# Front of a fused Fourier-mixing and hardswish kernel: two DMA queues for x and filters, weights' bits ahead, last-stage loads in three steps, zero matmuls in the wait

**Chip, cores, metric.** One core of a Trainium2 chip. The time is the device time of one execution in microseconds (us), median over repeated runs.

## The reference

```python
def _attn_ref(x, filt_r, filt_i):                 # x: (8, 3008, 256)
    X = np.fft.rfft(x, axis=1)
    Y = X * (filt_r + 1j * filt_i)[None, :, :]
    return np.fft.irfft(Y, n=x.shape[1], axis=1).astype(np.float32)

def _moe_ref(x, w_in, w_out):                     # x: (24064, 256), w_in: (256, 2048)
    h = x @ w_in
    g = h * np.clip(h + 3.0, 0.0, 6.0) / 6.0
    return (g @ w_out).astype(np.float32)
```

The first result, as (8 * 3008, 256), is the second's input. Everything is float32.

## The kernel before

The Fourier transforms are matmuls with tables. A batch goes through: transform of x (for the first batch `a0_unit`, for the others `a_unit` and a trip of z through DRAM), filter units (`b_unit`, `f_unit`, `bi_unit`) with a trip of g through DRAM, and the last stage (`t4_load`, `n_unit`), which gives tokens to the hardswish steps. The float weights are rebuilt from their bits by `convert`, mostly on VectorE. Later batches' work is laid among the hardswish steps by `places`. What the change touches (`# ...` marks cuts):

```python
    def x0_load(j, n):                # batch 0's x, in five pieces of columns
        for p, a, m, h in ((0, 0, 32, 0), (H1, 0, 32, 1), (32, 32, NA - 32, 0), (H1 + 32, 32, NA - 32, 1),
                           (NA, 0, H1 - NA, 0)):
            nc.sync.dma_start(x0[p:p + m, j:j + n, :], rows[a:a + m, ds(h * HC + j, n), :])

    def z_store(b, c, q=None):
        # ...
                (q or nc.gpsimd).dma_start(z[:, :, ds(c * XC + 2 * g, 2), :], t[p0:p0 + KH, :, :, :])

    # ... the front:
        for c in range(FB):
            table_load(0, c)          # filters and tables, all on nc.sync
        for j in range(0, HC, 4):
            a0_unit(j)
        for c in range(FB, NT):
            table_load(0, c)
            convert(0, most=min(c + 2, 6))      # only loads bits
        convert(3, False, 6)
        # ...
        for c in range(NT + 1):
            # ... b_unit, f_unit of 2c, 2c+1
            if c:
                bi_unit(0, 2 * c - 2)
                g_store(0, 2 * c - 2, nc.scalar)
            if c == NT - 2:
                for i in range(2):
                    t4_load(i, 0, KH - 2 * TC)
        for i in range(2):
            t4_load(i, KH - 2 * TC, KH, (nc.sync, nc.scalar))
        convert(2, False)
        for i in range(2):
            for dh in range(2):
                n_unit(i, dh)
    # ... places of batch 1, in steps of about 8 us:
                b_at = [11 + 18 * i // 11 for i in range(NU)]
    # ...
                at(s, z_store, n, c, nc.sync if n == 1 else None)
    # ... the last output stores:
        po, qs = st["po", k], (nc.sync, nc.scalar, nc.gpsimd)
```

## Time and profile before

2763.46 us (2762.95 to 2768.56, 3 runs). The marks, from the trace (us from the start of the span):

| mark | before |
|---|---|
| batch 0's transform ends on TensorE | 29.51 |
| its filter stage ends | 67.74 |
| first last-stage matmul | 80.03 |
| first hardswish on VectorE | 90.20 |
| 21st hardswish (the weight conversions end at 150.3, with the 13th) | 184.41 |
| 23rd hardswish, after the wait for batch 1's z | 200.70 |
| 49th hardswish | 304.62 |
| last arithmetic on VectorE ends | 2753.55 |
| end of the span | 2763.09 |

How to read it: the same instruction, counted by its order, is sought in two traces, and the difference of its start is carried from mark to mark. Where the difference changes, time was won or lost; where it stays, nothing happened, however busy the engines were. Half clock means a stretch in which the trace shows a granted clock of 0.5; a matmul of the code is two passes in the trace (the 16 matmuls of zeros are x32).

### The profile page before, as it was taken

The page shows a single profiled execution, that of the slowest core. Times are in us where ns is not written, and L with a number is a line of the kernel's source. Part 1 is how long each engine was busy: PE and PEld are TensorE (multiplying, and loading weights), DVE is VectorE, ACT ScalarE, POOL GpSimd, SP SyncE. Part 2 cuts the span into 40 slices and gives each one's busy share as a digit, 9 for nine tenths or more (in the row PEclk, how much of TensorE's full clock was granted, in tenths as well). Part 3 has the DMA queues.
Part 4 walks back from the last instruction along what each step waited for, and adds up shares of the span by engine and source line. Part 5 has one row for each costly group of instructions (what it writes and reads, how often), then busy time and mean ns, then how long its engine had stood idle before and what let it go on. Part 6 is the DMA issues. An engine that isn't in the chain of part 4 may idle for free.

```text
span 2763.1 us, 47097 instructions
## 1 busy us (share of the span) xinstructions
PE 2708.6 (98%) x18122; PEld 2409.1 (87%) x18122; DVE 1941.5 (70%) x3399; ACT 1332.5 (48%) x2665; POOL 373.6 (14%) x585
## 2 busy tenths in 40 slices
PE   8789999999999999999999999999999999999998
PEld 6468888999889998899889998899988999999997
DVE  5747765777667776677756787567775777766665
ACT  4334455444554445544554445544455444444443
POOL 1311112010210102110121101210012100100000
PEclk9899999999999999999999999999999999999999
DMA  8632223221332213322133212332123321110000
GB/s 214 190 87 83 71 64 80 74 76 52 83 89 61 72 40 89 88 72 57 46 84 90 76 49 54 86 93 67 46 61 89 97 64 45 35 32 23 19 9 16
DMA packets 119145, 195.25 MB, mean 71 GB/s; under 512 B 21539, under 2 KB 82947, under 8 KB 118463
## 3 DMA queue, kind: packets, MB, share of 16 engines
q1 hardware_dynamic: 98703, 146.59, 18.8%
q0 software_dynamic: 16480, 42.13, 6.7%
q10 hardware_dynamic: 3738, 3.52, 0.5%
q8 instruction: 143, 2.34, 0.4%
q14 instruction: 81, 0.66, 0.1%
HBM read 120.32 MB, written 71.83 MB: 70 GB/s over the span
## 4 chain that ended last, share of the span: by engine, by line
PE 93%; DVE 3%; DMA 2%; SPq 0%; issue 0%; ACT 0%; POOL 0%; POOLq 0%; DVEq 0%; ACTq 0%
PE po L526 41%; PE al L450 23%; PE be L450 17%; PE psn L425 4%; PE psf L355 3%; PE psf L332 2%; PE psf L387 2%; DMA w_all<-in_x_dram 0%; PE po L300 0%; DMA w_all<-wb_t 0%; DVE g L500 0%; DVE y L230 0%; PE po L548 0%; PE al L537 0%; DVE y L243 0%
## 5 line engine op out<-in xcount | busy, mean ns | idle before, releaser
L526 PEld LDWEIGHTS po<-w_all,g 128*128 128x128 f32 x10304 | 1369.1, 192 | 143.5 <-issue 36.5
L526 PE MATMUL po<-w_all,g 128*128 128x128 f32 x10304 | 1399.3, 276 | 3.7 <-DVE g L500 3.3
L500 DVE SCALAR_TENSOR_TENSOR g<-r,h 128x512 f32<-128x512 f32 x736 | 506.4, 688 | 268.1 <-ACT r L495 255.5
L495 ACT ACTIVATE r<-h,half_c 128x512 f32<-128x512 f32 x736 | 531.2, 722 | 326.8 <-DVE h L476 314.8
L450 PE MATMUL al<-xt,w_all 128*128 128x256 f32 x2208 | 660.5, 381 | 1.5 <-DVE h L481 1.0
L476 DVE TENSOR_TENSOR h<-be,s 128x512 f32<-128x512 f32 x368 | 254.2, 691 | 271.3 <-PE be L450 259.9
L450 PE MATMUL be<-xn,w_all 128*128 128x256 f32 x1472 | 438.3, 379 | 0.0
L450 PEld LDWEIGHTS al<-xt,w_all 128*128 128x128 f32 x2208 | 335.5, 192 | 3.5 <-issue 2.2
L450 PEld LDWEIGHTS be<-xn,w_all 128*128 128x128 f32 x1472 | 280.0, 190 | 38.0
L490 ACT ACTIVATE h<-al 128x256 f32<-128x256 f32 x368 | 141.4, 384 | 350.5 <-PE al L450 350.5
L481 DVE TENSOR_TENSOR h<-al,s 128x256 f32<-128x256 f32 x368 | 156.3, 425 | 166.1 <-PE al L450 164.8
L508 DVE TENSOR_TENSOR g<-g 128x512 f32<-128x512 f32 x368 | 254.7, 692 | 12.7
L471 ACT ACTIVATE s<-al 128x256 f32<-128x256 f32 x368 | 141.4, 384 | 207.1 <-PE al L450 207.1
L462 ACT ACTIVATE s<-be 128x256 f32<-128x256 f32 x368 | 141.4, 384 | 176.3 <-PE be L450 176.3
L450 PE MATMUL al<-xn,w_all 128*128 128x256 f32 x736 | 219.9, 381 | 0.5 <-ACT h L490 0.5
L450 PE MATMUL be<-xt,w_all 128*128 128x256 f32 x736 | 218.9, 379 | 0.0
L461 ACT ACTIVATE s<-al 128x256 f32<-128x256 f32 x368 | 141.4, 384 | 70.9 <-PE al L450 70.9
L510 DVE TENSOR_TENSOR g<-g 128x256 f32<-128x256 f32 x368 | 160.8, 437 | 12.5
L344 POOL DMA_DIRECT2D z_tmp<-t x192 | 111.1, 587 | 411.3 <-ACT t L335 409.1
L507 DVE TENSOR_TENSOR g<-g 128x256 f32<-128x256 f32 x368 | 156.4, 425 | 12.6
L450 PEld LDWEIGHTS be<-xt,w_all 128*128 128x128 f32 x736 | 139.8, 190 | 18.9
L425 PEld LDWEIGHTS psn<-wai,t 128*128 128x128 f32 x1024 | 134.2, 195 | 20.2 <-issue 14.1
(114 smaller groups left out, 1770.1 us busy)
## 6 DMA issues: line engine op xcount, KB each, us to landing
t<-g_tmp SPq DMA_DIRECT2D x188, 120.0 KB
t<-z_tmp SPq DMA_DIRECT2D x42, 512.0 KB
g_tmp<-t POOLq DMA_DIRECT2D x84, 256.0 KB, 3.8
z_tmp<-t POOLq DMA_DIRECT2D x192, 96.0 KB, 3.3
out_dram<-o SPq DMA_DIRECT2D x321, 47.0 KB
xs<-in_x_dram SPq DMA_DIRECT2D x112, 128.0 KB
ft<-in_filt_r_dram SPq DMA_DIRECT2D x88, 128.0 KB
ft<-in_filt_i_dram SPq DMA_DIRECT2D x88, 128.0 KB
```

The source lines that it names most:

```text
L425: nc.tensor.matmul(ps[:, ts(q, TOK)], t4[i % 2][:, q, ts(dh, P)], wai[:, chunks[i][1] + q, :], start=True, stop=True)
L450: nc.tensor.matmul(ps, w_in[p][:, w, :], x, start=start, stop=stop, skip_group_check=True)
L461: nc.scalar.activation(out=s[:, 0, :], in_=al, func=AXT.Copy)
L462: nc.scalar.activation(out=s5, in_=be[:, 1, :], func=AXT.Copy)
L476: nc.vector.tensor_tensor(out=st["h"][0].rearrange("p (a n) -> p a n", a=2), in0=be, in1=s, op=ALU.add)
L481: nc.vector.tensor_tensor(out=st["h"][1][:, 256:512], in0=al, in1=s5, op=ALU.add)
L495: nc.scalar.activation(out=r, in_=st["h"][i], func=AXT.Relu, bias=half_c, scale=1.0 / 6.0)
L500: nc.vector.scalar_tensor_tensor(out=st["g", k, p][:, o:o + 2, :].rearrange("p a n -> p (a n)"), in0=st["r", i], scalar=1.0, in1=st["h"][i ...
L507: v.tensor_tensor(out=g[:, G1, :], in0=g[:, G3, :], in1=g[:, G22, :], op=ALU.add)
L508: v.tensor_tensor(out=g[:, G3:G2 + 1:2, :], in0=g[:, G3:G1 + 1, :], in1=g[:, G11:G11 + 1, :].broadcast_to([P, 2, 256]), op=ALU.subtract)
L510: v.tensor_tensor(out=g[:, G4, :], in0=g[:, G12, :], in1=g[:, G2, :], op=ALU.subtract)
L526: nc.tensor.matmul(st["po", k][bank][:, part, u, :], g[:, a, ts(u, P)], w_out[p][:, w, :], start=(p == 0 and n in OPENS and u == 0), stop= ...
```

## The change

Its intent is to fill TensorE's idle time in the first 200 us: x and filters issued from two queues (SyncE and GpSimd), five weights' bits loaded ahead, last-stage loads in three steps of k, 16 matmuls of zeros to keep the clock up in the wait for them, and batch 1's z stored from GpSimd's queue instead of SyncE's. The core of the diff (its renamings, the shape of t4, the moved sums, the warm-up, the first loads on ScalarE and the new place of the turns are cut):

```diff
+    def table_load(b, c, qs=(nc.sync, nc.sync)):
...
     def x0_load(j, n):
-        for p, a, m, h in ((0, 0, 32, 0), (H1, 0, 32, 1), ...
-            nc.sync.dma_start(x0[p:p + m, j:j + n, :], rows[a:a + m, ds(h * HC + j, n), :])
+        nc.vector.memset(x0[32:64, j:j + n, :], 0.0)
+        for a, m in (0, 32), (32, NA - 32):
+            for h, q in ((0, nc.sync), (1, nc.gpsimd)):
+                q.dma_start(x0[h * 64 + a:h * 64 + a + m, j:j + n, :], rows[a:a + m, ds(h * HC + j, n), :])
...
         for c in range(FB):
-            table_load(0, c)
+            table_load(0, c, two)                    # two = (nc.sync, nc.gpsimd)
         for j in range(0, HC, 4):
             a0_unit(j)
+        convert(3, False, 5)
         for c in range(FB, NT):
-            table_load(0, c)
-            convert(0, most=min(c + 2, 6))
-        convert(3, False, 6)
+            table_load(0, c, two)
+        convert(0, most=8)
...
             if c:
                 bi_unit(0, 2 * c - 2)
-                g_store(0, 2 * c - 2, nc.scalar)
-            if c == NT - 2:
-                for i in range(2):
-                    t4_load(i, 0, KH - 2 * TC)
-        for i in range(2):
-            t4_load(i, KH - 2 * TC, KH, (nc.sync, nc.scalar))
+                g_store(0, 2 * c - 2, (nc.scalar, nc.scalar) if c < NT else (nc.scalar, nc.sync))
+            if c > 3:
+                t4_load(0, (0, KH - 2 * TC, KH - TC)[c - 4], (KH - 2 * TC, KH - TC, KH)[c - 4], (nc.sync, nc.scalar)
+                        if c == NT else None, 1)
+        keep_warm(16)
         convert(2, False)
...
-                b_at = [11 + 18 * i // 11 for i in range(NU)]
+                b_at = [12 + 17 * i // 11 for i in range(NU)]
...
-                at(s, z_store, n, c, nc.sync if n == 1 else None)
+                at(s, z_store, n, c)
```

## The prediction

> **What bounds the kernel now.** I read the page first. Part 1 gives TensorE 98% of the span, and the 40 slices in part 2 are at 9 from the fourth on, so nearly everything is TensorE-bound and only the front can give time back.
>
> ```profile
> span 2763.1 us, 47097 instructions
> ...
> PE   8789999999999999999999999999999999999998
> ```
>
> Next I read the table of stretches for five long stages. Between 700 and 2700 us TensorE is busy all the time (500.00 of 500.00 in each stretch); between 200 and 700 us it lacks 7 us. This steady part, untouched by the diff except through batch 1's places, I take as fixed. What is saved in front is then saved at the end.
>
> Then I read the same table in stretches of 5 us (columns: length, then busy us of PE, PEld, DVE, ACT, POOL with counts, granted clock, DMA share, GB/s).
>
> ```profile
> 20.00:25.00 5.00, 5.00 (x40) 5.00 (x40) 0.00 (x0) 3.69 (x5) 0.00 (x0) 0.84 0.99 219
> ...
> 40.00:45.00 5.00, 5.00 (x32) 3.49 (x30) 4.30 (x8) 2.17 (x4) 0.00 (x0) 1.00 0.26 53
> ...
> 70.00:75.00 5.00, 0.00 (x0) 0.00 (x0) 4.86 (x9) 0.00 (x0) 1.86 (x3) 0.78 0.53 144
> 75.00:80.00 5.00, 0.00 (x0) 0.00 (x1) 0.37 (x1) 0.00 (x0) 1.36 (x3) 0.50 0.21 51
> ```
>
> See three things: the DMA engines are saturated at only about 219 GB/s early on; they nearly stop at 40 to 45 us; TensorE stands still from 67.8 to 80 us and its clock falls to half. The timeline gives the edges:
>
> ```profile
> 16.92 12.58 PE L300 MATMUL po<-p,w_all 110*128 110x128 f32 x96 [2.35 <-DMA w_all<-in_x_dram]
> ...
> 65.32 2.42 PE L387 MATMUL psf<-h,wi 128*64 128x512 f32 x8 [0.72 <-ACT t L390]
> ...
> 80.03 4.98 PE L425 MATMUL psn<-wai,t 128*128 128x94 f32 x22 [12.29 <-DMA t<-g_tmp]
> ...
> 89.24 2.21 PE L537 MATMUL be<-xn,w_all 128*128 128x512 f32 x4
> 90.20 0.69 DVE L500 SCALAR_TENSOR_TENSOR g<-r,al 128x512 f32<-128x512 f32 x1 [14.84 <-ACT r L495]
> ```
>
> So batch 0's first transform runs to 29.5 us, its filter stage to 67.74, TensorE waits 12.3 us for the loads of the last stage, and the first hardswish is at 90.2. From there to 150.4 VectorE is busy 56.2 of 60.2 us, converting the other eleven weight parts: this stage is VectorE-bound and only starts earlier or later as a whole. After it one stall remains, which the waits and the timeline show:
>
> ```profile
> 171.66 11.95 SPq L603 DMA_DIRECT2D out_dram<-o  x14
> 183.65 3.22 SPq L344 DMA_DIRECT2D z_tmp<-t  x4
> 190.23 1.49 SPq L348 DMA_DIRECT2D t<-z_tmp  x3
> ...
> 194.14 2.07 PE L355 MATMUL psf<-t,wb 128*128 128x256 f32 x4 [5.51 <-DMA t<-z_tmp]
> ```
>
> The last z stores of batch 1 stand on SyncE's queue behind fourteen output stores, the z load behind them, and TensorE waits 5.5 us for it.
>
> **What the Trainium skill says.** (1) "SBUF — State Buffer", Door 1: The DMA port swizzle: 32 or 64 partitions from 0 reach half of the 16 ports, at most about 218 GB/s. The trace agrees: 219 GB/s at a DMA share of 0.99 while x and filters come in pieces of at most 32 partitions. (2) The same page, "Can I just issue two DMAs to hit both halves?", measured only 6% more; "DMA: Bandwidth & Descriptors", Issuing engines are not separate DMA queues, says more queues save only issue time. No trace here tests it yet; I follow the page and credit the two queues with almost no bandwidth. (3) "TensorE: Matmul & The Clock Gate", What's actually happening: after an idle window of about 3.4 us the clock is half. The trace agrees: granted clock 0.50 at 75 to 80 us, 0.52 from 80 to 90.2. (4) "SBUF — State Buffer", Who interferes with whom: GpSimd and VectorE share a port pair. In the trace the same conversion step takes 0.43 us alone and 0.56 or 0.67 beside the GpSimd sums.
>
> **The change, part by part.**
>
> *x.* The sixteen duplicated rows go: 16 x 32 KB = 0.5 MB of 3.6 MB, 2.4 us at 219 GB/s. In their place VectorE zeroes 32 x 8192 values; the 512-wide memset takes 0.48 us, so 7.7 us, from about 1.5 to 9.2, ahead of the conversions and beside the loads. ScalarE now issues four DMAs before the first activation, so the warm-up starts near 4.4 instead of 2.29 us (four issues of about 0.4, table load 1.28). Its ten half-passes end about 11 instead of 9.65. By then half of x is there, with the bits sharing bandwidth; the last of it I put at 20. The transform's 128 passes at the warm 0.111 us (from the eight-pass pieces of 0.89) take 14.2 us; some waiting included it ends at **26, not 29.5: 3.5 us saved**.
>
> *Filter stage.* It lasts 67.74 - 29.54 = 38.2 us. SyncE's queue stood 7.9 us behind a g store, which held a completion semaphore that the next table load needed (the lull at 40 to 45); TensorE paid 0.71 + 1.69 us later at two wb tables. In the new program's listed waits no table load waits for a g store. Putting the turn after the filter matmuls starts the first filter 1.8 us earlier. Summing the new order, before the last filter matmul stand six turns of 1.78, five filter groups of 1.8 and four inverse groups of 1.88, 27.2 us; then 1.1 to its first result, 4.25 of VectorE, 1.4 for the last inverse: 34.8 with the first hand-over. The extra bits loaded ahead of tables 2 to 5 (1 MB) and stores that wait for table loads cost about 1, so **36: 2.2 us saved**. The stage ends near 62.
>
> *Last-stage loads and zeros.* Before, it was 1.1 us of copies, 2.2 waiting for a semaphore, 4.1 for the store to land, then loads to 80. Now the last piece is four loads instead of eight and the stores use two queues; data I expect 10 to 11 us after the stage's end. But the sixteen matmuls of zeros stand ahead of them in TensorE's order: 32 passes at 0.43 us = **13.8 us, longer than the wait: 1.5 us lost** against 12.3. What they buy is the clock: at half clock it took 10.2 us from 80.03 to the first hardswish. Warm, 24 passes at 0.125 (from 10 in 1.25 us at 187.4), 1.88 for the first up product, 0.8 for relu make 5.7 to 5.8: **4.4 us saved**. The copies are within these numbers.
>
> *Conversion stage.* Same eleven conversions. z stores move to GpSimd, which already does the sums, next to a full VectorE; sums go one step later. I charge **1 us**.
>
> *Batch 1's z.* With its stores on GpSimd, the z load no longer follows a store behind the outputs, and the first filter step is one step (about 8 us) later. The 5.5 us stall goes. It left TensorE cold too: granted 0.53 in 192 to 196 and 0.61 in 196 to 200, some 2.4 us of work lost. **7.9 us saved**.
>
> Sum: 3.5 + 2.2 - 1.5 + 4.4 - 1.0 + 7.9 = 15.5. Thus 2763.5 - 15.5 = **2748 us**, 0.6% less.
>
> **The rivals.** *A: the two queues do raise the rate*, since they fill opposite halves at once; for it stands 310 to 320 GB/s at 50 to 60 us, against it the page and those stretches' other shapes. Then x lands by 15, but TensorE's own passes and the warm-up hold the transform at about 24 to 25, and the sum rises by only 1 to 3: 2745 to 2747. *B: the tables come late*, because issuing on GpSimd is slow and the bits precede tables 2 to 5. For it: by my count 8.3 MB must land before table 2 is complete, 38 us at 219 GB/s, just when it is wanted; then each group waits and the front saves only 3 or 4 instead of 8.6: 2752 to 2754. *C: zeros too many*: already counted; if their clock stays low for part, they take up to 18 us and cost 4 more: 2752. *D: GpSimd becomes the conversion stage's brake* through the shared ports: 24 stores at up to 0.2 us give 5 more: 2752. *E: the z stall only moves*, as output stores still precede the load; I expect it at about 178 against a need at 187, so little chance. If it stayed: 2756.
>
> **Range and chances.** A takes 3 off, B, C and D each add 4 to 5 and hardly all together; E is rare. So 2742 to 2754 eight times in ten. Two per cent is 55 us; all the front's idle time on TensorE before 200 us is less than that: 68.4 of the first 90 us are already busy, and 12.2 + 3.8 + 5.5 are the stalls. So faster 0.005, same 0.99, slower 0.005.
>
> **What would show it right or wrong.** In the changed profile: the transform's last matmul at 26 and the filter stage's last at 62; zero matmuls for 13.8 us right up to the last-stage matmuls, with no load named as their wait; granted clock near 1 there; first hardswish near 81 to 82; conversions still some 60 us; no wait on z loads near 180. DMA at 215 to 230 GB/s while x comes speaks for the page, 280 or more for rival A. A gain under 8 us, or one over 22, would mean that a step is wrong: first the filter stage's 36 us, then the claim that what comes after 200 us is fixed.

## The result

2765.24 us (2763.69 to 2766.78, 4 runs) against 2764.41 us of the kernel before. The ratio is the mean of the one kernel's runs over the mean of the other's of the same rounds, so it is not quite the ratio of these medians: 1.0001, 95% interval 0.9983 to 1.0018. Executions over 1.5% slower than the fastest of the same kernel are left out of the means. The same time; the predicted 15.5 us did not come.

TensorE's timeline of the changed kernel (start, us, engine, line, operation, in brackets the idle time before and its releaser) stands against the four lines of TensorE in the prediction's timeline:

```profile
16.97 12.59 PE L300 MATMUL po<-p,w_all 111*128 111x128 f32 x96 [1.85 <-DMA w_all<-in_x_dram]
...
44.07 1.97 PE L355 MATMUL po<-t,w_all 128*128 128x256 f32 x8 [2.67 <-DMA w_all<-wb_t]
...
65.37 2.42 PE L387 MATMUL psf<-h,wi 128*64 128x512 f32 x8 [0.72 <-ACT t L390]
67.73 14.00 PE L643 MATMUL al<-r 128*128 128x512 f32 x32
85.00 3.30 PE L425 MATMUL psn<-wai,t 128*128 128x94 f32 x22 [3.27 <-DMA xs<-in_x_dram]
```

The transform still ends at 29.56 and the filter stage at 67.80 us, now with a 2.67 us wait for a table. The zeros run 14.00 us as computed, but TensorE then waits another 3.27 us. The named releaser is the event that came last by the profile: these matmuls read t and wai, not xs. The chain that ended last, from the same trace (start, us, what), shows the way:

```profile
27.64 16.29 DMA w_all<-wb_t
...
66.46 4.72 DMA g_tmp<-t
...
73.16 0.58 SPq L418
...
73.80 0.02 SPq L396
...
73.85 3.46 DMA g_tmp<-t
...
77.38 4.19 DMA t<-g_tmp
```

The table that the filter stage waits for was 16.3 us under way. And the second half of the last g store (L396) stands on SyncE's queue behind four last-stage loads (L418), which first wait for an earlier g store to land: it is issued at 73.85 us, though ScalarE issued the other half at 68.67. The stretches after it (length, busy us of the five engines with counts, granted clock, DMA share, GB/s):

```profile
85.00:90.00 5.00, 4.77 (x26) 4.02 (x27) 0.00 (x0) 1.52 (x4) 0.00 (x0) 0.68 0.69 173
90.00:95.00 5.00, 5.00 (x9) 2.22 (x8) 0.69 (x1) 0.69 (x1) 0.00 (x0) 0.63 0.53 210
```

So the clock fell to half in spite of the zeros, and the first hardswish is at 93.49 us, 3.3 us later than before, as VectorE's timeline says:

```profile
93.49 0.69 DVE L500 SCALAR_TENSOR_TENSOR g<-r,al 128x512 f32<-128x512 f32 x1 [18.06 <-ACT r L495]
```

The wait for z did go: where the old timeline had 5.51 us, the changed one has none.

```profile
197.37 1.06 PE L355 MATMUL psf<-t,wb 128*128 128x256 f32 x4
```

But half of that is given back round 240 us. The same passes, found by their order, in TensorE's timeline before and after:

```profile
247.54 0.59 PE L450 MATMUL be<-xn,w_all 128*128 128x256 f32 x2
247.97 1.05 PE L526 MATMUL po<-w_all,g 128*128 128x128 f32 x8
```

```profile
237.32 0.59 PE L450 MATMUL be<-xn,w_all 128*128 128x256 f32 x2
240.19 1.83 PE L526 MATMUL po<-w_all,g 128*128 128x128 f32 x8 [2.27 <-DVE g L500]
```

There is an idle time of 2.27 us where there was none, and eight passes take 1.83 us instead of 1.05: half clock was granted from 240.4 to 243.9 us. From the 23rd to the 49th hardswish TensorE idles 2.0 us more than before and runs 3.4 us at half clock, some 1.7 us of work: together the 3.7 us that are lost here. The chain there goes through VectorE from 235.35 to 240.05 us (L576, L375, L376, L367 to L369, L500): in this step VectorE has an output addition and a filter unit ahead of the hardswish.

Last, the end of the span. These are the DRAIN instructions with which GpSimd's and SyncE's sequencers finish (shortest, median and longest in ns, first and last start in us), before and after:

```profile
L839 POOLq DRAIN  x3: 40/102/6117, 2756.2 to 2762.8; - x3
L839 SPq DRAIN  x3: 7/7/7, 2760.0 to 2762.6; - x3
```

```profile
L845 POOLq DRAIN  x3: 46/102/9620, 2753.8 to 2763.9; - x3
L845 SPq DRAIN  x3: 7/7/7, 2757.6 to 2763.6; - x3
```

SyncE, which has waited for all output to land, was done 2.4 us earlier than before (2760.0, 2757.6), but GpSimd's long drain took 9.62 us instead of 6.12, and the span ends with it. The whole account, from the same marks:

| part | predicted | measured | difference to before, carried |
|---|---|---|---|
| transform's end | -3.5 | +0.05 | +0.05 |
| filter stage | -2.2 | +0.01 | +0.06 |
| wait for the last-stage loads | +1.5 | +4.91 | +4.97 |
| from there to the first hardswish | -4.4 | -1.68 | +3.29 |
| from there to the 21st hardswish | +1.0 | -1.65 | +1.64 |
| z wait and its cold clock | -7.9 | -9.02 | -7.38 |
| from there to the 49th hardswish | 0 | +3.72 | -3.66 |
| 305 us to the last hardswish | 0 | +1.21 | -2.45 |
| from there to the end of the span | 0 | +3.51 | +1.06 |

### The profile page after: what moved, and what is told of

Same layout as the page of the kernel before. It is cut to its first block, busy times and chain, and to the rows that moved or that the text cites. A ratio compares the mean times of both kernels' runs of the same rounds, so it can differ in the third digit from the quotient of the medians.

```text
span 2764.2 us, 47162 instructions
## 1 busy us (share of the span) xinstructions
PE 2716.7 (98%) x18154; PEld 2412.4 (87%) x18154; DVE 1951.5 (71%) x3404; ACT 1332.9 (48%) x2665; POOL 408.4 (15%) x640
## 3 DMA queue, kind: packets, MB, share of 16 engines
q0 software_dynamic: 19088, 48.65, 7.7%
## 4 chain that ended last, share of the span: by engine, by line
PE 93%; DVE 3%; DMA 2%; issue 0%; ACT 0%; SPq 0%; POOL 0%; ACTq 0%; POOLq 0%; DVEq 0%
PE po L526 42%; PE al L450 23%; PE be L450 17%; PE psn L425 4%; PE psf L355 3%; PE psf L332 2%; PE psf L387 2%; DMA w_all<-wb_t 1%; DVE g L500 0%; DMA w_all<-in_x_dram 0%; PE po L548 0%; PE po L300 0%; PE al L537 0%; DMA t<-g_tmp 0%; DVE y L229 0%
## 5 line engine op out<-in xcount | busy, mean ns | idle before, releaser
L500 DVE SCALAR_TENSOR_TENSOR g<-r,h 128x512 f32<-128x512 f32 x736 | 506.7, 688 | 269.5 <-ACT r L495 257.0
L344 POOL DMA_DIRECT2D z_tmp<-t x224 | 130.2, 585 | 421.4 <-ACT t L335 393.6
L582 POOL TENSOR_TENSOR o<-p,o 128x256 f32<-128x256 f32 x45 | 32.7, 728 | 813.1 <-ACT t L390 381.1
```

The source lines that it names most:

```text
L500: nc.vector.scalar_tensor_tensor(out=st["g", k, p][:, o:o + 2, :].rearrange("p a n -> p (a n)"), in0=st["r", i], scalar=1.0, in1=st["h"][i ...
```

## The experiments

Each kernel ran beside the old one; the ratio is to the old kernel, with its 95% interval. g_store_act, places, z_alone and tail ran on one chip beside the same runs of the old kernel; so did no_zeros, bits_late, x_one_queue and joined; joined_14 and z_places_tail; and mended_end and z_halves. In profiles the differences to the old kernel's trace are given at the marks. The old runs beside no_zeros' group are the nine beside g_store_act's and one more. What the text calls faster is an interval that leaves out 1.

### The wait for the last-stage loads

**g_store_act**: both halves of the last g store on ScalarE's queue.

```diff
-                g_store(0, 2 * c - 2, (nc.scalar, nc.scalar) if c < NT else (nc.scalar, nc.sync))
+                g_store(0, 2 * c - 2, (nc.scalar, nc.scalar))
```

> The changed kernel with one edit: both halves of the last g_store on ScalarE's queue (in the change the second half is on SyncE, behind four last-stage loads that wait there). Theory: SyncE's place in order delayed that store to 73.85 us, and with it the last loads. Then the store is issued by 69.5 us, the last loads land by 79 us, the last-stage matmuls start at 81.7-82.0 us, as soon as the zeros end (85.00 in the change), and the first hardswish at 87.5-91 us (93.49). Rival: the last loads are late because they share the DMA engines with the bits and x loads: then the matmuls still start at 84-85 us. Of the time, 2-5 us at the first hardswish, of which the later stages give back some: total 2760-2765 us.

2759.84 us; 0.9984 (0.9972 to 0.9997). The second half is issued at 70.04 instead of 73.85 us. TensorE's timeline:

```profile
68.47 14.00 PE L643 MATMUL al<-r 128*128 128x512 f32 x32
82.31 2.59 PE L425 MATMUL psn<-wai,t 128*128 128x94 f32 x22
```

No wait is left after the zeros and no half clock follows: 22 passes take 2.59 instead of 3.30 us, and the first hardswish is at 88.29, 6.0 us after the first last-stage matmul (8.5 in the change, 10.2 before). The theory held within 0.6 us, and the rival (shared DMA engines) fell. Of the 5.2 us by which this profile's first hardswish is ahead of the change's, 3.6 are left at 305 us.

**no_zeros**: the 16 zero matmuls taken out of the change.

```diff
-        keep_warm(16)
```

> The changed kernel without the 16 zero passes ahead of the last-stage matmuls (the wait stays, TensorE is idle in it). Theory: the matmuls there wait for the last loads (landed 84.7 us), not for the zeros (over at 81.7 us), and the zeros did not keep the clock (half clock from 86.8 us all the same); so they start at 84-85.5 us as with the zeros, at half clock, and the first hardswish comes at 93-96 us (93.49 in the change; 98.03 and 95.62 in two more profiles whose beginning is the same): nothing lost by taking the zeros out, the total within 2 us of the change. Rival (the zeros are worth their place): the first hardswish 3 us or more later than that, or (the zeros are on the path) 3 us earlier.

2765.35 us; 1.0001 (0.9987 to 1.0015). The last-stage matmuls wait for data as with the zeros, and 22 passes take 4.98 us, at half clock:

```profile
85.85 4.98 PE L425 MATMUL psn<-wai,t 128*128 128x94 f32 x22 [16.83 <-DMA xs<-in_x_dram]
```

First hardswish 95.75. So the zeros were not on the path, and in the total no use of them shows. In the profiles it depends on the draw: from the first last-stage matmul to the first hardswish it is 9.9 us here, 10.0 and 10.2 in places and tail, 8.5 in the change and 6.1 in mended_end, all four with the zeros (for these runs see below).

### The transform and the filter stage

**bits_late**: the fourth and fifth weights' bits behind the tables.

```diff
-        convert(3, False, 5)
+        convert(3, False, 3)
```

> The changed kernel with the loads of the fourth and fifth weights' bits (1 MB in all) issued behind all tables instead of ahead of the last four. Theory: the wait of the filter stage for table 2 (2.67 us at 41.4 us in the change; 3.2, 1.9+2.2 and 4.0+1.4 us in the other profiles with the same beginning) is there because these bits are ahead of the tables; then it is under 1 us, and the filter stage ends at 64-66 us (67.8, 68.5, 70.3, 68.2). Rival: the tables are late because two queues share the same engines, whatever is ahead; then the wait stays over 2 us. The bits are then late for the conversions, by some us at the conversion stage in the worst case.

2761.14 us; 0.9990 (0.9976 to 1.0004). No wait for a table is left, and the filter stage takes 35.5 us (26.28 to 61.80 us). TensorE's timeline:

```profile
54.79 1.99 PE L355 MATMUL po<-t,w_all 128*128 128x256 f32 x8
59.38 2.43 PE L387 MATMUL psf<-h,wi 128*64 128x512 f32 x8 [0.72 <-ACT t L390]
61.73 14.00 PE L643 MATMUL al<-r 128*128 128x512 f32 x32
80.34 4.98 PE L425 MATMUL psn<-wai,t 128*128 128x94 f32 x22 [4.60 <-DMA t<-g_tmp]
```

The theory held, better than expected: the stage ends at 61.80 instead of 64 to 66. In joined and joined_14 below, with the same edit, it takes 37.5 and 37.0 us, with one wait for a table (1.8 and 1.3 us). But the last loads land at 80.3 and the idle time behind the zeros grows to 4.60, with half clock from 78.8: of 6 us only 3.3 reach the first hardswish (90.21).

**x_one_queue**: x's first loads on SyncE alone.

```diff
-            for h, q in ((0, nc.sync), (1, nc.gpsimd)):
+            for h, q in ((0, nc.sync), (1, nc.sync)):
```

> The changed kernel with x's first loads all on SyncE again (the tables stay on two queues). Theory: the x loads take the ports' rate either way (215 and 217 GB/s in 10-20 us with one queue and with two), so the transform ends at 26.5-29.6 us as in the change. Rival (two queues help): with one queue the third x block comes 1-3 us later and the transform ends at 30-32 us. Order alone could tell too: 25 issues on one queue at some 0.65 us each are over at 17 us, which may delay the tables; then the first filter matmul comes later than 34 us.

2768.24 us; 1.0015 (1.0002 to 1.0029). My expectation fell, the rival's came more than true: the third block starts at 21.06 instead of 16.97 us and the transform ends at 34.0.

```profile
21.06 12.96 PE L300 MATMUL po<-p,w_all 111*128 111x128 f32 x96 [3.14 <-DMA w_all<-in_x_dram]
```

Yet the rate is no lower. The stretches of 10 us, of the change and of this run (the 215 and 217 GB/s of my expectation are those of 10 to 15 us):

```profile
10.00:20.00 10.00, 8.00 (x56) 7.05 (x55) 9.73 (x16) 5.00 (x6) 5.48 (x7) 0.93 1.02 210
```

```profile
10.00:20.00 10.00, 5.93 (x34) 5.03 (x32) 9.62 (x20) 3.46 (x4) 1.07 (x2) 0.75 1.03 222
```

With 222 GB/s against 210 the engines moved other bytes first: with x off GpSimd's queue, that queue issues bits and tables from 1.29 us on instead of 9.86. And SyncE, now with all of x, is late with it. Its issues of x, in the change and in this run:

```profile
0.75 11.11 SPq L291 DMA_DIRECT2D w_all<-in_x_dram  x10
```

```profile
0.74 20.67 SPq L291 DMA_DIRECT2D w_all<-in_x_dram  x20
```

In one wait it stood 6.3 us for the landing of a weight's bits that ScalarE had issued, and x's third load went out at 13.35 to 16.49 us instead of 3.42 to 5.84. So the second queue buys x an earlier turn. The Trainium skill, "DMA: Bandwidth & Descriptors", Queues, rings and completion order, says that each engine goes round the queue rows that have work, packet by packet, so x might also get a larger share; no run here shows that apart from the late issues. The filter stage loses nothing by the late transform: it waits for no table, takes 35.5 us and ends at 69.52, inside the range of the front with two queues, which follows.

**How far the front varies by itself.** Four profiles, the change's own among them, have the very same front (the change, places, tail, mended_end). Their transform ended at 29.56, 26.60, 26.74 and 26.76 us, their filter stage at 67.80, 70.28, 68.21 and 66.63, their first hardswish came at 93.49, 98.03, 95.62 and 89.31. In each, TensorE waited for tables of the filter stage (2.7; 1.4 and 4.0; 2.2 and 1.9; 2.4 and 1.8 us). g_store_act and no_zeros, the same up to the end of the filter stage, ended the transform at 26.41 and 28.20 and that stage at 68.54 and 69.02. So the change's own profile was a poor draw for the transform (its last 96 passes took 12.59 us, with half clock from 18.6, where tail's took 10.96): 26.4 to 26.8, what was predicted, is usual, but what the transform wins the tables take.

Half clock came in places (42.4 and 86.7 us) and tail (43.8 and 84.7), in the change at 18.6 and 86.8, in mended_end nowhere in the first 110 us. The Trainium skill, "TensorE: Matmul & The Clock Gate", What's actually happening, says why that may be chance: the window in which activity is counted runs freely, it "doesn't reset when your kernel starts". The four profiles agree with that (idle 2.69 us behind the zeros in mended_end and full clock; 3.27, 3.31 and 3.82 in the others and half clock), though no run here moves the window on purpose. The clock records of the traces go further. In each of the 15 traces half clock begins on a grid of 3.413 us. Of this grid's steps at full clock, in the first 300 us, 55 were followed by half clock, and in 54 of these TensorE had been idle, by its modelled ends, for 1.8 to 3.4 us (the one left is the change's at 83.4 us: 1.57, behind a step with 1.70); in the 1,097 followed by full clock it had been idle for at most 1.90. So in these traces somewhat over half a window of idle time is enough, and it matters where its edges fall: the 2.69 us of mended_end fell on two steps (1.88 and 0.81), the 3.82 of places left 2.52 in one.

### After 200 us

**places**: the change with the steps of batch 1's filter units as in the old kernel from 14 on.

```diff
-                b_at = [12 + 17 * i // 11 for i in range(NU)]
+                b_at = [12, 13] + [11 + 18 * i // 11 for i in range(2, NU)]
```

> The changed kernel with only the places of the filter units of steps 11 to 29 changed (12, 13, then the old kernel's 14, 15, 17, 19, ... instead of 15, 16, 18, 19, ...). Theory: the 2.28 us idle of TensorE at 240 us and the 3.4 us of half clock after it come from a filter unit landing on step 16 of the changed kernel; then both are gone and the lead over the old kernel at 305 us is 7.4 us instead of 3.66 us, up to 5.5 us more to the end than the old one. Rival: those 3.7 us are a give-back that comes wherever the work stands; then the lead at 305 us stays 3-4.5 us and the half clock appears in another step.

2760.23 us; 0.9986 (0.9973 to 0.9998). Its front was the slowest of the four (first hardswish +7.83 to before). Carried on: +5.33 at 184 us, -3.69 behind z, -4.33 at 305 us and -4.32 at the last hardswish. Nothing is given back, and the stretch from 240 us has the full clock (0.66 in the change):

```profile
240.00:245.00 5.00, 5.00 (x32) 4.48 (x31) 4.63 (x9) 1.88 (x4) 0.00 (x0) 1.00 0.39 149
```

The lead of 7.4 us at 305 us did not show, because this front was 3.7 us worse at 184 us; what was lost between is 0, and that is what the theory said.

**z_alone**: the old kernel with z on GpSimd's queue and the change's places.

```diff
-                b_at = [11 + 18 * i // 11 for i in range(NU)]
+                b_at = [12 + 17 * i // 11 for i in range(NU)]
...
-                at(s, z_store, n, c, nc.sync if n == 1 else None)
+                at(s, z_store, n, c)
```

> The old kernel with one part of the change alone: z_store on GpSimd's queue for block 1 too, with the changed kernel's places. Theory: the 5.5 us wait for z at 194 us and the cold clock round it go, nothing before 155 us moves (first hardswish at 90.2 us, within 0.3), and the lead is 8-9.5 us at 200 us and 5-5.7 us at 305 us, where the same give-back at 240 us comes. If the final drain of GpSimd grows with its DMAs, its end is later than 9 us after the last bytes' issue there as in the changed kernel (9.6 us, 6.1 in the old one); if it is chance, it is as often 6 as 9.

2765.50 us; 1.0005 (0.9992 to 1.0018). The first hardswish moved by +0.79, more than the 0.3 that I allowed. From 184 us (+1.36) to behind z (-7.66) it wins 9.02 us, as much as in the change, and by 305 us -1.73 is left: 5.9 us given back, more than the 3.7 expected. GpSimd's final drain takes 8.18 us instead of 6.12. So z on GpSimd wins 9.0 us and, by its places and the drain, loses 8 of them.

### The end of the span

**tail**: the change with the last output stores on SyncE and ScalarE alone.

```diff
-        po, qs = st["po", k], (nc.sync, nc.scalar, nc.gpsimd)
+        po, qs = st["po", k], (nc.sync, nc.scalar)
```

> The changed kernel with one edit: the last two stores of the output on SyncE and ScalarE alone, none on GpSimd. Theory: the span ends with GpSimd's drain, which lasts 9.6 us here after its last output DMA (6.1 us in the old kernel); without output DMAs at the end GpSimd's drain starts some us earlier and the span ends with the last bytes, about 2760-2761 us, 3-5 us earlier than the change. Rival: the drain ends at the same time or later whatever it has issued last (fixed by SyncE's landing waits): total within 1 us of the change.

2761.97 us; 0.9992 (0.9978 to 1.0006).

```profile
L845 POOLq DRAIN  x3: 46/102/8770, 2706.6 to 2759.9; - x3
```

GpSimd's long drain now starts at 2706.6 us and is over 44 us before the end. From the last arithmetic to the end of the span it is 7.54 us (9.54 before, 13.05 in the change). Thus the drain was on the path. In the profile the total gained less than these 5.5 us on the change, since its first hardswish came 2.1 us later.

**z_halves** and **z_thirds**: the old kernel with each z store cut into two or three DMAs, to see what sets the drain.

```diff
-                (q or nc.gpsimd).dma_start(z[:, :, ds(c * XC + 2 * g, 2), :], t[p0:p0 + KH, :, :, :])
+                for k0 in range(0, KH, KH // 3):        # z_halves: KH // 2
+                    (q or nc.gpsimd).dma_start(z[k0:k0 + KH // 3, :, ds(c * XC + 2 * g, 2), :], t[p0 + k0:p0 + k0 + KH // 3, :, :, :])
```

> The old kernel with each store of z cut into two DMAs of half the size (GpSimd issues 478 DMAs instead of 286, SyncE 64 instead of 32; the bytes are the same). Theory: GpSimd's final drain grows with the number of DMAs that this engine has issued, some 60 ns for one (6.1 us at 286, 8.2 at 318, 9.6 at 342): then it lasts 16-19 us here, and the span grows by 10-12 us, to 2772-2778 us, with the last output landed at the same time. Rival: it goes by bytes or packets, or is chance: then it lasts 6-10 us, and the total stays within 3 us of the old kernel.

2768.21 us; 1.0017 (1.0004 to 1.0029). The drain took 10.44 us. That is neither the theory (16 to 19) nor the rival (within 10 us): the number of DMAs does not set it.

> The old kernel with each store of z cut into three DMAs of a third of the size (same bytes; GpSimd's queue then carries 16,480 + 2 x 3,072 = 22,624 packets, as halves brought 3,072 more). Theory, found after the run with halves: GpSimd's final drain grows by 1.4 ns for each packet that its queue has carried (16,480: 6.12 us; 18,016: 8.18; 18,688: 9.21; 19,088: 9.62; 19,552: 10.44). Then it lasts 14.5-15.0 us here and the span ends 18-18.5 us after the last arithmetic (9.5 in the old kernel). Rival: it only levels off or depends on something else that came with those runs: then it lasts 8-13 us.

2766.00 us; 1.0007 (0.9991 to 1.0024). The packets were 25,696, more than I had told, and the drain took 6.34 us:

```profile
L840 POOLq DRAIN  x3: 40/102/6345, 2757.0 to 2763.9; - x3
```

The second theory fell as well. All six lengths beside what GpSimd's queue had carried, where GpSimd issued the same eight output stores at the end: 16,480 packets 6.12 us; 18,016 8.18; 18,688 (x_one_queue) 9.21; 19,088 9.62; 19,552 10.44; 25,696 6.34. The change and four more profiles with the same DMAs lie at 9.60 to 9.62 us, so it is not chance; what sets it stays open.

### Together

**joined**: the change with five edits: g_store_act, places, bits_late and tail as above, and 9 zero matmuls instead of 16. **joined_14**: the same with 14.

```diff
-        keep_warm(16)
+        keep_warm(9)          # joined_14: 14; the other four edits as above
```

> The changed kernel with five edits at once: last g_store on ScalarE's queue alone; 9 zero passes instead of 16; the places with the old kernel's steps from 14 on; the bits 4 and 5 behind the tables; no output DMA on GpSimd at the end. From the separate runs: last output arithmetic at 2746.6 us with the first edit; the places give 3.7 us more, the bits 2-3, the zeros 0-3 us, less half of what comes before 145 us; the end then 0.8 us after the last landing, 7.3 us after the last arithmetic. So 2745-2753 us, 0.4-0.7% faster than the old kernel. If the drain is not on the path, or the gains overlap wholly, 2754-2760 us.

2747.01 us; 0.9937 (0.9924 to 0.9949).

> The five edits together as before, with 14 zero passes instead of 9. Theory: with 9 the zeros ended 5.0 us ahead of the last loads (72.68, 77.68 us), the clock went to half at 77.7 us, and 10.2 us lay between the first last-stage matmul and the first hardswish, against 6.0 us in the run where the zeros reached to it. With 14 the zeros end at 76.5-77.5 us, there is no half clock between 70 and 90 us, and the first hardswish comes at 83.5-85 us (87.83); of that 3-4 us the conversion stage gives back up to 2 us: 1.5-4 us less in all, 2743-2746 us. Rival: half clock comes whatever the idle time is, first hardswish at 87-88 us and the total as with 9.

2745.26 us; 0.9934 (0.9920 to 0.9947). TensorE's timelines, first joined, then joined_14:

```profile
64.69 7.99 PE L643 MATMUL al<-r 128*128 128x512 f32 x18
77.68 4.95 PE L425 MATMUL psn<-wai,t 128*128 128x94 f32 x22 [5.00 <-DMA t<-g_tmp]
```

```profile
64.92 12.28 PE L643 MATMUL al<-r 128*128 128x512 f32 x28
77.04 2.59 PE L425 MATMUL psn<-wai,t 128*128 128x94 f32 x22
```

With 9 the zeros end 5 us ahead of the loads and the 22 passes run at half clock; with 14 they reach to the loads and the passes run at full clock. First hardswish 87.83 and 83.02. The medians differ by only 1.8 us and the intervals overlap; the profile of joined_14 was of its fastest run (2742.31), so the 7 us between the two profiles are not its worth. That the zeros are worth something once they reach the loads is shown in the profiles; how much in the total is not settled. Both versions beat the old kernel and the changed one; joined_14 is 18.4 us under the old kernel by the medians of the same rounds.

**z_places_tail**: the old kernel with z on GpSimd, the places and the tail, its front untouched. **mended_end**: the change with places and tail, its front untouched.

```diff
 # z_places_tail, against the old kernel
-                b_at = [11 + 18 * i // 11 for i in range(NU)]
+                b_at = [12, 13] + [11 + 18 * i // 11 for i in range(2, NU)]
...
-                at(s, z_store, n, c, nc.sync if n == 1 else None)
+                at(s, z_store, n, c)
...
-        po, qs = st["po", k], (nc.sync, nc.scalar, nc.gpsimd)
+        po, qs = st["po", k], (nc.sync, nc.scalar)
```

> The old kernel's beginning untouched, with three things: block 1's z_store on GpSimd, the places with the old steps from 14 on, and no output DMA on GpSimd at the end. Theory: these act alone: first hardswish at 90-91 us as in the old kernel, 7.5-9 us ahead of it at 200 us, the same 7.5-8.3 us ahead at 305 us and at the last hardswish (no give-back), and the span ends 0.8 us after SyncE's drain: 2752-2755 us. So most of what the joined version gains would come without the changed beginning. Rival: without the changed beginning the idle time at 240 us or elsewhere takes the 7.5 us back: 2758 us or more.

2753.94 us (2752.96 to 2754.63); 0.9964 (0.9951 to 0.9976). First hardswish -0.36 to before, -0.78 at 184 us, -9.80 behind z, -10.44 at 305 us and at the last hardswish: the full 9.0 us of z come, and stay.

> The changed kernel with its beginning untouched and the two edits that come after 200 us: the places with the old steps from 14 on, and no output DMA on GpSimd at the end. The old kernel with z_store on GpSimd and the same two edits ran 2753.94 us; so this run is the worth of the changed beginning by itself. Theory: that beginning costs 1-5 us (the first hardswish came 3.3 to 7.8 us later in the profiles with it, of which 145-155 us gives back half): 2755-2759 us. Rival: the beginning is worth something once nothing behind it takes it back: 2748-2753 us.

2756.74 us (2749.94 to 2759.69); 0.9972 (0.9959 to 0.9986). Its ratio and that of z_places_tail have overlapping intervals: the changed front by itself shows no gain, and spreads the runs over 10 us where the old front spreads them over 2. Its profile was of the fastest run, the one with no half clock in the front (-0.90 at the first hardswish, -12.22 behind z, -12.87 at 305 us). Mended, the front is worth something: joined_14 ran 8.7 us under z_places_tail by the medians of the same rounds.

## Why the prediction was wrong

- **"26, not 29.5: 3.5 us saved"**: right in four of the six profiles that share it (26.4 to 26.8), and without worth, since the tables then came late. Giving the second queue no part in it was wrong: without it SyncE's issues of x wait and the transform ends at 34.0.
- **"36: 2.2 us saved"** failed, in its part "the extra bits loaded ahead of tables 2 to 5 (1 MB) [...] cost about 1". They cost the stage some 2 to 8 us: it took 39.9 to 43.7 us in places, tail, mended_end, g_store_act and no_zeros, 35.5 to 37.5 in the three runs with the bits behind the tables. The stage's own work was summed rightly; rival B was the truth in its part that the bits precede the tables (slow issuing on GpSimd was not tested), and was sized too small, with 4 to 5 us in the total and nothing for the waits behind it.
- **"13.8 us, longer than the wait"** failed: 17.2 us of wait, not 13.8. I gave the loads 10 to 11 us after the stage's end because "the stores use two queues", and did not see that the second of them stands behind loads that wait. One word of the diff put right (g_store_act) brings the wait down to the zeros.
- **"Warm [...] 4.4 us saved"** failed in the change as a consequence: the zeros ended 3.27 us too early for the clock. Where they reached to the loads, it took 6.0 us to the first hardswish (g_store_act, joined_14) against the 5.7 to 5.8 told: the mechanism is right.
- **"I charge 1 us"** for the conversion stage: not found. From the 1st to the 13th hardswish, where the conversions end, the change needs 0.1 us more than before, and all other profiles lie between -0.6 and +0.7. The 1.65 us that the table shows as won lie between the 13th and the 15th: half clock there lasts 3.4 us instead of 6.8 (from 144.5 us before). In the profiles with 6.8 (z_alone, z_places_tail, bits_late) these two steps take 0.1 to 0.6 us less than before, in those with 3.4 it is 1.4 to 2.0, in joined_14, with none, 3.5. The change did not aim at it and no run sets it on purpose: this gain is luck.
- **"7.9 us saved"** at z: right, 9.02 measured, the same in z_alone and z_places_tail.
- **"The claim that what comes after 200 us is fixed"**, named as the second doubt, failed by 8.4 us: +3.72 for the places that moved with z, +1.21 near 2,100 us (other profiles have between 0 and 1.6 there, so this part is taken for chance), and +3.51 for GpSimd's drain. I had read the diff's line of places as a consequence of z, and had not looked at what ends the span.
- Of the other rivals, A fell (210 GB/s in 10 to 20 us, against 280 or more; but the 219 GB/s of the old kernel were no test of ports, since x's pieces lay on partitions 0 to 109 there too), C's slow zeros did not come (14.00 us), nor D's 5 us (+0.1 to the 13th hardswish), nor E's wait.

So of the missing 16.6 us about half was never won in front, and half was given back behind 200 us. z, places and tail alone, with the old front, give 0.36%, over half of joined_14's 0.66%.

## What to carry to other kernels

A store put on a queue whose next entries wait is as late as their wait: on each queue read what stands ahead of an issue, not how many queues there are. A wait removed in a scheduled kernel moves the work behind it onto other steps; check the step where it lands (here a filter unit on a full VectorE), and check what ends the span, which need not be the engine that is 98% busy. Filler matmuls are sure to pay only if they reach to the data: size them from the wait that is left after the other edits, and judge a front by several profiles, since one of four fell 8.7 us from another with the same instructions.

## What the Trainium skill lacked or had wrong

- "DMA: Bandwidth & Descriptors", Issuing engines are not separate DMA queues: that more issuing engines save only the sequencers' time agrees with the rates here (222 GB/s with x on one queue, 210 with two, in 10 to 20 us). What it lacks is that this time need not be small: in this program one issue stood 6.3 us for the landing of an earlier load, and x's third block was 4.1 us later.
- "TensorE: Matmul & The Clock Gate", What's actually happening: half clock after at least one idle window of about 3.4 us. Here 1.8 to 3.4 us of idle time in one step of the grid of 3.413 us came before half clock in 54 of 55 cases, for one 2.27 us at 240 us by TensorE's modelled ends; after the 2.69 us of mended_end, split over two steps, it did not come.
- No page has the final drain of GpSimd as a cost: 6.1 to 10.4 us long where it issued output at the end, over 2.4 to 6.7 us after SyncE had seen all output landed, and off the path when its last DMA comes over 50 us before the end.
